# Second layer of the last three token tiles by seven block products in place of eight, with sums of W_out's blocks kept in DRAM

## The chip, the cores and the metric

One core of a Trainium2 chip runs the whole kernel. TensorE (PE in the profile; its weight loads are the row PEld) multiplies, VectorE (DVE), ScalarE (ACT) and GpSimd (POOL) do the rest, and SyncE (SP) and ACT issue the transfers. The metric is the device time of one execution in microseconds, the median of several runs.

## The reference

Block-sparse attention over 4 batches, 8 heads, 768 tokens and 64 features a head, then a feed-forward with two weight matrices on the 3072 x 512 result:

```python
scores = np.where(mask, scale * np.matmul(q, k.transpose(0, 1, 3, 2)), -1e9)   # block mask, 32 x 32 blocks
attn = np.exp(scores - max); attn = attn / (attn.sum(-1, keepdims=True) + 1e-9)
x = np.matmul(attn, v).transpose(0, 2, 1, 3).reshape(3072, 512)
h = x @ w_in                                                     # 512 -> 2048
sp = np.where(h > 20.0, h, np.log1p(np.exp(np.minimum(h, 20.0))))
out = (h * np.tanh(sp)) @ w_out                                  # 2048 -> 512
```

## The kernel before, in words

Attention runs as 52 jobs, 13 a batch: two blocks of 32 queries a job, with a dense job for the first and the last block of a batch. A job's scores (tile s) need its keys gathered by POOL into one of three buffers (kg0 to kg2, L598) and its values gathered by SP from DRAM (vg<-vd); then come maximum, exponential, transposes (t), score-weighted values (obank), a division and a transpose back (tx), and the result is stored in two half-precision parts, xh and xl.

The feed-forward works on 12 tiles of 256 tokens, three a batch, written 0_0 to 3_2. Everything in it is a pair of float16 parts, a high part and a remainder, and a product of two such pairs takes three matmuls (high x high, high x low, low x high). The first layer (`moe_h`, L1049) makes h of a tile in 8 pieces of two steps; a step is 12 matmuls of 256 columns, and its weights change with every matmul. Two pieces make one quarter k of a tile: 512 of the 2048 hidden features, laid out as 4 chunks of 128 on the partitions. The activation (`moe_g`) of a quarter is a chain: two copies of h out of PSUM (hs, ACT L1060), exponential (us, ACT L1078), a minimum and an addition (DVE L1081), a square (POOL L1083 or ACT L1084), a logarithm and an exponential (ACT L1085, L1086), the product with hs (DVE L1087), the cast to float16 (g's high part, DVE L1096 or ACT L1094), and the remainder (POOL L1099).

The second layer (`moe_y`, L1114) takes, for each half m of 128 tokens, the 16 chunks of W_out (`wo`, 512 columns each) times g: 48 matmuls of 512 columns into one PSUM bank, in steps of 6 matmuls; 96 a tile. Then the bank is scaled into ys (DVE or ACT, L1126 and L1128) and sent out (SP, L1132). The second layer of a tile runs between the first-layer steps of the tile that follows; that of the last tile runs alone at the end, first half of the tokens before the second.

The order on every engine is fixed when the program is built, by a planner (`Plan`): each piece of work is added with an engine (or several to choose from), an estimated length, what it reads and writes, and a rank; the planner places them one after the other by these estimates, with rings of buffers as limits (`RINGS`). Semaphores are put in afterwards from the tiles that instructions read and write; in PSUM they keep two engines apart by bank. A step of the feed-forward is ready work for PE whenever an attention step is not; the feed-forward's steps keep their own order. W_out is decoded and split into its two parts before the feed-forward needs it, and stays in SBUF.

Of the kernel before, what the change touches and what calls it, by code (L numbers as in the profile page):

```python
# [21 lines left out]
PSC = 4096.0  # L22
# [186 lines left out]
def attn_mish_kernel(ctx: ExitStack, tc: tile.TileContext, qT, kT, v, sampled, blocks, w_in, w_out, out):  # L209
# [11 lines left out]
    nc = tc.nc  # L221
    P = 128
# [99 lines left out]

    sb = ctx.enter_context(tc.tile_pool(name="attn", bufs=2))
    ps = {n: ctx.enter_context(tc.tile_pool(name=f"ps_{n}", bufs=RINGS[n], space=PSUM)) for n in "sthy"}
# [17 lines left out]
    NKG, NVG = 2, 3  # L342
    kgs = [const.tile([P, 2 * NPR, KT], F16, name=f"kg{n}") for n in range(NKG)]
    vgs = [const.tile([P, 2, H, VW], F16, name=f"vg{n}") for n in range(NVG)]
    RAW = H * VW
    T3 = range(NTT)

    def squares(src, out):

        n = src.free_size()  # L350
        junk = sb.tile([P, 4 * TT], F16, name=nc.get_next_instruction_name(), tag="jk", bufs=1)
        nc.scalar.activation(out=junk[:, 0:n], in_=src, func=AF.Square, scale=float(2.0 ** -SQ), accum_out=out)
# [112 lines left out]
    def parts(b, what, j, cls):  # L465
# [15 lines left out]
        def hi():  # L481
            if first:
                new(sb, "kt", kt, [P, 2 * NPR, S], F16)
            elif what == "q":
                new(sb, "q", key, [P, 2 * NPR, TT], F16)
            raw, h, _ = views()
            nc.scalar.activation(out=h, in_=raw, func=AF.Copy, scale=tl[ks])
# [13 lines left out]
        if (what, b, j) in APART:  # L501
# [7 lines left out]
            def hi_of(eng):  # L509
                if first:  # L510
                    new(sb, "kt", kt, [P, 2 * NPR, S], F16)
                elif what == "q":
                    new(sb, "q", key, [P, 2 * NPR, TT], F16)
# [155 lines left out]
    def attend(job):  # L669
# [52 lines left out]
        def ex_fn(n):  # L722
            if n == 0:
                for k in kps:
                    new(sb, "pt", k, [P, S] if dense else [P, 2, 2, KT])
            pt, nb = tl[kp], tl["nb", i]
# [22 lines left out]
        def ph_fn(j):  # L749
            nc.scalar.activation(out=new(sb, "ph", ("ph", i, j), [P, 2, 2, P], F16), in_=tl["t", i, j], func=AF.Copy,  # L750
                                 scale=PSC)

        def pl_fn(j):
            nc.vector.scalar_tensor_tensor(  # L754
                out=new(sb, "pl", ("pl", i, j), [P, 2, 2, P], F16), in0=tl["t", i, j], scalar=PSC,
                in1=tl["ph", i, j], op0=ALU.mult, op1=ALU.subtract)
# [5 lines left out]
        def plf_fn(j):  # L762
            nc.scalar.activation(out=new(sb, "pl", ("pl", i, j), [P, 2, 2, P], F16), in_=tl["t", i, j], func=AF.Copy,
                                 scale=PSC)
# [40 lines left out]
        def xs_fn():  # L805
# [3 lines left out]
            nc.vector.reciprocal(out=r, in_=r)  # L809
            xs = new(sb, "xs", ("xs", i), [P, nsu, 2, D])  # L810
            nc.vector.tensor_tensor(
# [129 lines left out]
    def add_split(key, kg, a0, hi, lo, r, ring, cls, sc, ks, by_pe):  # L941
# [15 lines left out]
        if not by_pe:  # L957
# [20 lines left out]
            also=[("DVE", 0.68, lambda: cast("DVE", lo), False)])  # L978

    def a0_o(fc):  # L980
        return wo[:, fc].rearrange("p t d -> p (t d)").bitcast(F32)
# [85 lines left out]
    def moe_g(st, k, part):  # L1067

        b, t = st
        kq, ku, kg, kp = ("hs", b, t, k, part), ("us", b, t, k, part), ("g", b, t, k), ("gp", b, t, k, part)  # L1070
        n, c = (TT, 1.0) if part is None else (TT // 2, 0.56)
# [18 lines left out]
        def g_fn(eng):  # L1090
# [8 lines left out]
        add("POOL", 2.3 * c, lambda: nc.gpsimd.tensor_tensor(out=g(1), in0=hs(), in1=g(0), op=ALU.subtract),  # L1099
            r=[kq, ("gh",) + kp], w=[kp], use=[kg])  # L1100

# [35 lines left out]


    DL = 10
    jobs = []  # L1140
# [19 lines left out]
    def open_mlp():  # L1160
        wpool_cm.__exit__(None, None, None)
        pools["cm"] = tc.tile_pool(name="mlp", bufs=2)
        pools["m"] = pools["cm"].__enter__()

    LPE = 4
# [60 lines left out]
    for i, job in enumerate(jobs):  # L1226
# [32 lines left out]
    for st in order + [None]:  # L1259
        ys = [(m, k) for m in range(TT // P) for k in range(NFC // 4)] if prev else []  # L1260
        if st in HALVES:
            for n in range(NFP):
                moe_h(st, n, 0)
        for n in range(NFP):
            if st:
                moe_h(st, n, 1 if st in HALVES else None)
            if ys:
                moe_y(prev, *ys[n], st is None)
        prev = st
# [43 lines left out]
    FILL = 14.0, 200.0  # L1313
    plan.emit(pace, fill)
    pools["cm"].__exit__(None, None, None)

# [41 lines left out]
```

## Time and profile before

| what | value |
|---|---|
| median of 3 runs | 789.04 us (788.4 to 790.24) |
| span of the profiled execution, first to last instruction | 786.6 us |
| the median less that span | 2.4 us |
| instructions | 30628 |
| second-layer matmuls (L1114), 512 columns | 1152 |
| first-layer matmuls (L1049), 256 columns | 2304 |

The page gives the span of the profiled execution and no other time of it; the 2.4 us are what the timed runs hold on top. A busy PE in the profile is not PE at its peak, since matmuls overlap: the mean length of one (380 ns for 512 columns) is longer than the distance from the start of one to the start of the next. Idle time is put down to what ended it.

### The profile page before, as it was taken

What the parts mean: (1) busy time and instruction counts of PE and PEld (TensorE: products, weight loads), DVE (VectorE), ACT (ScalarE), POOL (GpSimd) and SP (SyncE); (2) the same over time, 40 slices, a digit from 0 to 9 for tenths busy, and PEclk for the clock granted to TensorE, in tenths of its full rate; (3) what the DMA queues carried; (4) which work ended last, traced back from release to release, by engine and by line L of the source; (5) the groups of instructions that cost most, each with busy time, mean ns of one, the idle gap of its engine ahead of it and who ended that gap; (6) DMA issues with size and microseconds to landing.
All of it is one profiled execution on the core that took longest, in us unless ns stands there. A gap on an engine that the chain in (4) does not pass through costs nothing.

```text
span 786.6 us, 30628 instructions
## 1 busy us (share of the span) xinstructions
PE 740.5 (94%) x12793; PEld 518.7 (66%) x12793; DVE 493.5 (63%) x900; ACT 542.7 (69%) x880; POOL 307.6 (39%) x393
## 2 busy tenths in 40 slices
PE   6677899888999999999999999999999999999997
PEld 5544578665577767767776676677677667666663
DVE  6868988998767764795866457656665453223220
ACT  3555778768868877777887768786876666455650
POOL 2114244887635542374443422534641331213021
PEclk9989999999999999999999999999999999999999
DMA  9878857104534475244346603523444112000000
GB/s 339 263 236 256 268 176 202 44 2 136 159 117 131 119 198 171 69 162 120 87 139 194 192 15 101 174 77 91 119 115 119 37 39 81 14 15 14 14 14 27
DMA packets 57742, 95.31 MB, mean 121 GB/s; under 512 B 8323, under 2 KB 20612, under 8 KB 57604
## 3 DMA queue, kind: packets, MB, share of 16 engines
q1 hardware_dynamic: 52032, 80.51, 34.9%
q10 hardware_dynamic: 5572, 12.85, 4.8%
q8 instruction: 100, 1.64, 0.9%
q14 instruction: 38, 0.31, 0.1%
HBM read 80.38 MB, written 12.95 MB: 119 GB/s over the span
## 4 chain that ended last, share of the span: by engine, by line
PE 73%; DVE 10%; ACT 6%; DMA 5%; issue 2%; POOL 1%; SPq 1%; POOLq 1%; ACTq 0%; DVEq 0%
PE h_None L1049 27%; PE y L1114 26%; PE obank L789 6%; PE t L667 6%; PE s L661 4%; DMA vg<-vd 3%; PE tx L667 1%; PE wd_i L947 1%; DVE wt_o L965 1%; DMA wr<-in_moe_w_in_dram 1%; DVE hs_None L1087 1%; DVE v L491 1%; DMA raw_k<-in_k_dram 1%; ACT us_None L1078 1%; POOL kt L522 1%
## 5 line engine op out<-in xcount | busy, mean ns | idle before, releaser
L1049 PE MATMUL h_None<-xh,wi 128*128 128x256 f16 x1536 | 282.8, 273 | 0.0
L1114 PE MATMUL y<-wo,g 128*128 128x512 f16 x1152 | 278.0, 380 | 4.0 <-POOL wo L970 2.6
L1049 PEld LDWEIGHTS <-wi 128*128 128x128 f16 x2304 | 223.5, 98 | 47.3 <-issue 2.1
L1049 PE MATMUL h_None<-xl,wi 128*128 128x256 f16 x768 | 209.8, 273 | 0.0
L1114 PEld LDWEIGHTS <-g 128*128 128x128 f16 x1152 | 111.1, 98 | 106.7 <-issue 7.3
L1099 POOL TENSOR_TENSOR g<-hs_None,g 128x1024 f16<-128x1024 f32 x48 | 107.6, 2241 | 188.4 <-DVE g L1096 144.8
L598 POOL COPY kg<-kt 128x256 f16 x258 | 107.2, 451 | 123.3 <-PE s L661 109.7
L1060 ACT ACTIVATE hs_None<-h_None,gsc 128x512 f32<-128x512 f32 x96 | 65.5, 684 | 80.2 <-PE h_None L1049 79.4
L727 ACT ACTIVATE pt<-s,nb,ns 128x256 f32<-128x256 f32 (+1 forms) x208 | 106.3, 582 | 5.7 <-PE t L667 5.0
L750 ACT ACTIVATE ph<-t 128x512 f16<-128x512 f32 x112 | 66.5, 596 | 45.1 <-PE t L667 45.0
L754 DVE SCALAR_TENSOR_TENSOR pl<-t,ph 128x512 f16<-128x512 f32 x105 | 71.9, 686 | 35.8 <-ACT ph L750 35.5
L1087 DVE SCALAR_TENSOR_TENSOR hs_None<-us_None,hs_None 128x1024 f32<-128x1024 f32 x48 | 65.0, 1355 | 40.1 <-ACT us_None L1086 40.1
L667 PE MATMUL t<-ident,pt 128*128 128x128 f32 x448 | 70.4, 280 | 6.8 <-DVE pl L754 3.6
L708 DVE TENSOR_REDUCE mx<-s 128x4 f32<-128x1024 f32 x44 | 53.7, 1222 | 31.9 <-PE s L661 31.3
L1083 POOL TENSOR_TENSOR us_None<-us_None 128x1024 f32<-128x1024 f32 x22 | 44.2, 2007 | 71.8 <-DVE us_None L1081 68.7
L667 PEld LDWEIGHTS t<-ident,pt 128*128 128x128 f32 x448 | 51.6, 142 | 21.4 <-DVE pl L754 4.5
L789 PEld LDWEIGHTS <-ph 128*32 128x32 f16 x3584 | 47.9, 94 | 20.9 <-issue 13.1
L1078 ACT ACTIVATE us_None<-hs_None,hsc 128x1024 f32<-128x1024 f32 x48 | 55.2, 1150 | 0.9
L789 PE MATMUL obank<-vg,ph 128*32 128x65 f16 (+1 forms) x3200 | 50.6, 196 | 4.0 <-DMA vg<-vd 2.2
L1081 DVE TENSOR_SCALAR us_None<-us_None 128x1024 f32<-128x1024 f32 x48 | 37.4, 778 | 25.4 <-ACT us_None L1078 25.2
L1085 ACT ACTIVATE us_None<-us_None 128x1024 f32<-128x1024 f32 x48 | 50.7, 1056 | 1.6 <-POOL us_None L1083 0.8
L1086 ACT ACTIVATE us_None<-us_None 128x1024 f32<-128x1024 f32 x48 | 50.7, 1056 | 0.8
(199 smaller groups left out, 893.6 us busy)
## 6 DMA issues: line engine op xcount, KB each, us to landing
vg<-vd SPq DMA_DIRECT2D x320, 65.0 KB, 2.6
vg<-vd SPq DMA_DIRECT2D x80, 195.0 KB, 3.2
wr<-in_moe_w_in_dram ACTq DMA_DIRECT2D x8, 1024.0 KB, 7.4
vd<-v SPq DMA_DIRECT2D x12, 520.0 KB, 3.8
vg<-vd SPq DMA_DIRECT2D x12, 520.0 KB, 5.1
raw_k<-in_k_dram SPq DMA_DIRECT2D x12, 512.0 KB, 5.4
raw_q<-in_q_dram SPq DMA_DIRECT2D x12, 512.0 KB, 4.3
raw_v<-in_v_dram SPq DMA_DIRECT2D x12, 512.0 KB, 5.0
```

The lines of the kernel that those rows point to most:

```text
L598: nc.gpsimd.tensor_copy(out=dst, in_=tl["kt", b][:, :, ds(j, BS)])
L667: nc.tensor.matmul(out, src, ident, start=start, stop=stop, is_transpose=True)
L727: ex = lambda o, x, g, w: nc.scalar.activation(out=o, in_=x, func=AF.Exp, bias=nb[:, g, w:w + 1], scale=tl["ns", b, sus[w]["qb"] // TB][:, ...
L750: nc.scalar.activation(out=new(sb, "ph", ("ph", i, j), [P, 2, 2, P], F16), in_=tl["t", i, j], func=AF.Copy, scale=PSC)
L754: nc.vector.scalar_tensor_tensor(out=new(sb, "pl", ("pl", i, j), [P, 2, 2, P], F16), in0=tl["t", i, j], scalar=PSC, in1=tl["ph", i, j], op ...
L789: nc.tensor.matmul(o[cs, w, g, 0:v1 - v0], p[:, k, g, cs], vt[:, k, 2 * c + g, v0:v1], start=j == 0 and g == 0 and k == 0 and n == 0, stop ...
L1049: nc.tensor.matmul(h[:, f2, 0:n].rearrange("p (s q) -> p s q", q=BS), wi[:, fp, cc // 2, w, cc % 2, fs], x[:, s0:s0 + sn, cc], start=f2 == ...
L1060: nc.scalar.activation(out=tl[kq][:, 2 * (fp % 2):2 * (fp % 2) + 2, 0:n], in_=tl[kh][:, :, 0:n], func=AF.Copy, scale=gsc[:, fp:fp + 1])
L1078: nc.scalar.activation(out=us(), in_=hs(), func=AF.Exp, scale=hsc[:, b:b + 1])
L1087: add("DVE", 1.32 * c, lambda: nc.vector.scalar_tensor_tensor(out=hs(), in0=us(), scalar=-0.5, in1=hs(), op0=ALU.add, op1=ALU.mult), r=[ku ...
L1099: add("POOL", 2.3 * c, lambda: nc.gpsimd.tensor_tensor(out=g(1), in0=hs(), in1=g(0), op=ALU.subtract), r=[kq, ("gh",) + kp], w=[kp], use=[kg])
L1114: nc.tensor.matmul(tl[ky], tl["g", b, t, k][:, g, f, q], wo[:, fc, w], start=fc == 0 and n == 0, stop=fc == NFC - 1 and n == 2)
```

## The change

For the last three tiles, 3_0, 3_1 and 3_2, the second layer is done by a scheme with seven products of blocks for eight. Of each quarter k, g is a 2 x 2 arrangement of blocks (two halves of 128 tokens by two halves of 256 features), and so is W_out (two halves of 256 features by two halves of 256 columns). Seven products of one block each, some of them of sums of blocks, give the four output blocks after additions. A product is 6 matmuls of 256 columns (two chunks, three pairs of parts), 42 a quarter and 168 a tile. Each of the seven gathers over all four quarters in its own half of a PSUM bank; the banks are those of y, s and obank for tiles 3_0 and 3_1, and those of h and t for tile 3_2. Two products share a bank in three of four cases.

The sums of W_out's blocks are made once, while jobs 27 to 41 of attention run: for each of 8 pairs of chunks two additions on DVE, four on POOL (or DVE), a cast to the high part and a subtraction for the low part, and a store of 512 KB to DRAM by SP. When attention is over, its buffers are given up and a pool in their place (`late`) takes the sums back with 8 transfers (`to`). The sums of g's blocks (`sg`) are made for each quarter behind the activation chain: four additions into the tile us, a cast, a subtraction. For these three tiles the remainder of g and both steps of sg may go to DVE as well as to POOL or ACT. When the last quarter is through, the seven products are scaled and added into yz by two copies on ACT and seven instructions on DVE or POOL, in place of two scalings, and each half of the tokens is sent out as before. The steps of second and first layer are mixed in proportion to their estimated lengths. The key and value buffers of attention, and other tiles of it, move to a pool on the other side of SBUF; nothing else about them is changed. First layers are as they were.

```diff
+        if not fold:
+            return
+        ksg = ("sg", b, t, k)
+        def fold_g(eng):
+            x = lambda f, m: tl[kq][:, 2 * f:2 * f + 2, m * P:(m + 1) * P]
+            y = [tl[ku][:, n].rearrange("p (j q) -> p j q", j=2) for n in range(4)]
+            for o, a_, b_, op in ((S1, x(0, 1), x(1, 1), ALU.add), (S3, x(0, 0), x(0, 1), ALU.subtract),
+                                  (S2, y[S1], x(0, 0), ALU.subtract), (S4, x(1, 0), y[S2], ALU.subtract)):
+                eng.tensor_tensor(out=y[o], in0=a_, in1=b_, op=op)
+        add("DVE", 1.4, lambda: fold_g(nc.vector), r=[kq], w=[ku], port=True,
+            also=[("POOL", 2.5, lambda: fold_g(nc.gpsimd), True)])
...
+    NLATE, WHEN = 3, [27, 28, 29, 30, 31, 32, 40, 41]
+    PRODS = ((B11, None, B11, None), (B12, None, B21, None), (None, S1, None, F1), (None, S2, None, F2),
+             (None, S4, B22, None), (None, S3, None, F3), (B22, None, None, F4))
+    HL = ((0, 0), (1, 0), (0, 1))
+    def folded(rk, r, four, two, parts, keys, home, after, use=(), ring="ft", rush=0.0, free=()):
+        def sums():
+            for o, a, b in four:
+                nc.vector.tensor_tensor(out=o(), in0=a(), in1=b(), op=ALU.add)
+        def fold(eng):
+            x = [r()[:, n] for n in range(4)]
+            for o, a, b, op in two:
+                eng.tensor_tensor(out=x[o], in0=x[a], in1=x[b], op=op)
...
+        add("SP", 0.5, lambda: nc.sync.dma_start(out=folds[key], in_=flat(kt).bitcast(F16)),
+            r=[("fh",) + key, ("fl",) + key], w=[("fd",) + key], use=[kt], lat=2.5, kind=dma(2.0), key=8.0)
...
+    def back_wo(k, j):
+        kt = ("to", k, j)
+        add("SP", 0.5, lambda: nc.sync.dma_start(
+            out=new(pools["l"], "to", kt, [P, 2, 4, TT], F16).rearrange("p w t f -> p (w t f)"), in_=folds["o", k, j]),
+            r=[("fd", "o", k, j), "late"], w=[("toh", k, j)], new=[("to", kt)], lat=2.5, kind=dma(2.0), key=-2 + k)
+
+    def pair_y(st, final):
+        sets = [("h", 0), ("h", 1), ("t", 0), ("t", 1)] if final else [("y", 0), ("s", 0), ("s", 1), ("o", 0)]
...
+        where = {0: (0, 0), 1: (0, 1), 2: (1, 0), 3: (1, 1), 5: (2, 0), 4: (2, 1), 6: (3, 0)}
+        R = lambda i: bank(where[i][0])[:, where[i][1] * TT:(where[i][1] + 1) * TT]
+        seq_ = (0, 3, 1, 2, 5, 4, 6)
+        def product(k, i, head):
+            a, s_, bb, t_ = PRODS[i]
+            for j in range(2):
+                for n, (x, w) in enumerate(HL):
+                    if a is not None:
+                        lhs = tl["g", b, t, k][:, x, 2 * (a % 2) + j, (a // 2) * P:(a // 2 + 1) * P]
+                    else:
+                        lhs = tl["sg", b, t, k][:, x, s_, j * P:(j + 1) * P]
+                    rhs = wo_at(4 * k + j + 2 * (bb // 2))[:, w, (bb % 2) * TT:(bb % 2 + 1) * TT] if bb is not None else \
+                        tl["to", k, j][:, w, t_]
+                    nc.tensor.matmul(R(i), lhs, rhs, start=head and j == n == 0,
+                                     stop=k == NFC // 4 - 1 and j == 1 and n == 2, skip_group_check=True)
+        for k in range(NFC // 4):
+            for i in seq_ if k < NFC // 4 - 1 else (0, 3, 2, 5, 4, 6, 1):
...
+        def end():
+            copy(0, 0, 0)
+            acc(3, 0, 1, 0, 0)
+            copy(2, 1, 1)
+            acc(5, 1, 0, 0, 1)
+            both(0, 1, 1, 1)
+            both(1, 1, 1, 0)
+            acc(4, 0, 1, 0, 1)
+            acc(6, 1, 0, 1, 0)
+            out_(1)
+            acc(1, 0, 0, 0, 0)
+            out_(0)
...
+    late_ = order[len(order) - NLATE:]
+    plain = order[:len(order) - NLATE + 1]
+    add("SP", 0.0, open_late, r=[("xw", i) for i in range(nj)], w=["late"], key=-9)
...
+    for st in order[len(plain):] + [None]:
+        steps, end = pair_y(prev, st is None)
+        ys = [(0.66, x) for x in steps[:-1]] + [(0.66, lambda s_=steps[-1], e=end: (s_(), e()))]
+        mixed([(2.62, lambda n=n, st=st: moe_h(st, n, None)) for n in range(NFP)] if st else [], ys)
```

More of the change, by code (lines that the diff above doesn't have):

```diff
@@ L749, in ph_fn @@
         def ph_fn(j):
-            nc.scalar.activation(out=new(sb, "ph", ("ph", i, j), [P, 2, 2, P], F16), in_=tl["t", i, j], func=AF.Copy,
+            nc.scalar.activation(out=new(at_, "ph", ("ph", i, j), [P, 2, 2, P], F16), in_=tl["t", i, j], func=AF.Copy,
                                  scale=PSC)
@@ L1135, in moe_y @@
             add("SP", 0.4, out_fn, r=[kys], lat=2.0, kind=("dma", 1.1))
+    dma = lambda d, n=1: ("dma", d)
+    NLATE, WHEN = 3, [27, 28, 29, 30, 31, 32, 40, 41]
+    B11, B12, B21, B22 = range(4)
+    F1, F3, F4, F2 = range(4)
+    S2, S4, S3, S1 = range(4)
+    PRODS = ((B11, None, B11, None), (B12, None, B21, None), (None, S1, None, F1), (None, S2, None, F2),
[9 more added lines that the diff above has]
+                eng.tensor_tensor(out=x[o], in0=x[a], in1=x[b], op=op)
+        out = lambda n: parts()[n]
+        add("DVE", 1.3, sums, r=after, w=[rk], new=[(ring, rk)], use=use, key=rush)
+        add("DVE", 1.35, lambda: fold(nc.vector), w=[rk], use=[rk], key=rush, port=True,
+            also=[("POOL", 2.4, lambda: fold(nc.gpsimd), True)])
+        add("ACT", 1.07, lambda: nc.scalar.activation(out=out(0), in_=r(), func=AF.Copy), r=[rk, *free],
+            w=[keys[0]], new=home, use=[rk, *keys[2:]], key=rush, also=[("DVE", 0.75, lambda: nc.vector.tensor_copy(out=out(0), in_=r()), True)])
+        add("DVE", 1.2, lambda: nc.vector.tensor_tensor(out=out(1), in0=r(), in1=out(0), op=ALU.subtract), port=True,
+            r=[rk, keys[0]], w=[keys[1]], use=[rk, *keys[2:]], key=rush,
+            also=[("POOL", 2.25, lambda: nc.gpsimd.tensor_tensor(out=out(1), in0=r(), in1=out(0), op=ALU.subtract), True)])
@@ new lines, in attn_mish_kernel, with fold_w, flat @@
+    FOLD_W = ((F1, B12, B11, ALU.subtract), (F3, B22, B12, ALU.subtract), (F2, B22, F1, ALU.subtract),
+              (F4, B21, F2, ALU.subtract))
+    folds = {}
+    def fold_w(key, four, when):
+        kr, kt = ("fr",) + key, ("ff",) + key
+        folds[key] = dram.tile([P, 8 * TT], F16, name="_".join(str(x) for x in ("folds",) + key))
+        def flat(k):
+            return tl[k] if k in tl else new(sb, "raw", k, [P, RAW], cols=4 * TT)
+        r = lambda: flat(kr).rearrange("p (n f) -> p n f", n=4)
+        parts = lambda: [flat(kt).bitcast(F16).rearrange("p (w n f) -> p w n f", w=2, n=4)[:, n] for n in range(2)]
+        folded(kr, r, [(lambda o=o: o(r()), a, c) for o, a, c in four], FOLD_W, parts, [("fh",) + key, ("fl",) + key, kt],
+               [("raw", kt)], [(w, key[0], *at) for w in ("wh", "wl") for at in (
+                   [(key[1], n) for n in range(2)] if key[0] == "i" else [(4 * key[1] + key[2] + 2 * h,) for h in range(2)])] +
+               [("begun", when)], (), "raw", 8.0)
+        add("SP", 0.5, lambda: nc.sync.dma_start(out=folds[key], in_=flat(kt).bitcast(F16)),
+            r=[("fh",) + key, ("fl",) + key], w=[("fd",) + key], use=[kt], lat=2.5, kind=dma(2.0), key=8.0)
@@ L1163, in open_mlp, with open_late @@
         pools["m"] = pools["cm"].__enter__()
+    def open_late():
+        at_cm.__exit__(None, None, None)
+        pools["lcm"] = tc.tile_pool(name="late", bufs=2, side="right", reuse_waits="tile")
+        pools["l"] = pools["lcm"].__enter__()
     LPE = 4
```

137 lines of the change are left out of this document (116 added, 21 removed).

## The prediction

> **What bounds the kernel now.** I read the page first (busy shares and the slices), then a table by stage, the timeline of the last 27 us, and the waits of TensorE. The page:
>
> ```profile
> PE 740.5 (94%) x12793; PEld 518.7 (66%) x12793; DVE 493.5 (63%) x900; ACT 542.7 (69%) x880; POOL 307.6 (39%) x393
> ```
>
> A table by stage says more than the 94%. Columns: stretch, its length, busy time with instruction count of PE, PEld, DVE, ACT and POOL, granted clock, DMA share, GB/s.
>
> ```profile
> 380.00:600.00 220.00, 217.12 (x4237) 155.21 (x4226) 141.00 (x268) 168.27 (x286) 91.88 (x139) 1.00 0.42 119
> 600.00:666.00 66.00, 65.52 (x982) 45.47 (x981) 29.59 (x50) 41.41 (x62) 14.87 (x12) 1.00 0.25 69
> 666.00:759.60 93.60, 93.60 (x649) 63.30 (x647) 25.55 (x30) 50.80 (x55) 21.93 (x10) 1.00 0.04 12
> 759.60:786.60 27.00, 22.19 (x103) 9.72 (x100) 3.27 (x4) 6.38 (x7) 2.12 (x1) 0.96 0.08 29
> ```
>
> From 666 us, when attention is over, to 759.6 PE has not one idle moment, at full clock, while DVE is at 27%, ACT at 54% and POOL at 23%. From 380 to 600 PE idles 2.9 of 220 us. So from there to the end the time is PE's instruction stream, and whatever shortens it, with its operands on time, shortens the run one for one. The end itself (start, length, engine, line, operation; in brackets the idle time before and who ended it):
>
> ```profile
> 759.33 0.27 PE L1049 MATMUL h_None<-xh,wi 128*128 128x256 f16 x1
> 759.44 9.66 PE L1114 MATMUL y<-wo,g 128*128 128x512 f16 x44
> 759.64 0.69 ACT L1060 ACTIVATE hs_None<-h_None,gsc 128x512 f32<-128x512 f32 x1 [3.98 <-PE h_None L1049]
> 760.36 1.15 ACT L1078 ACTIVATE us_None<-hs_None,hsc 128x1024 f32<-128x1024 f32 x1
> 761.61 0.68 DVE L1081 TENSOR_SCALAR us_None<-us_None 128x1024 f32<-128x1024 f32 x1
> 762.32 1.06 ACT L1084 ACTIVATE us_None<-us_None 128x1024 f32<-128x1024 f32 x1 [0.81 <-DVE us_None L1081]
> 765.66 1.23 DVE L1087 SCALAR_TENSOR_TENSOR hs_None<-us_None,hs_None 128x1024 f32<-128x1024 f32 x1 [3.37 <-ACT us_None L1086]
> 767.78 2.12 POOL L1099 TENSOR_TENSOR g<-hs_None,g 128x1024 f16<-128x1024 f32 x1 [8.28 <-DVE g L1096]
> 769.96 12.69 PE L1114 MATMUL y<-wo,g 128*128 128x512 f16 x58 [0.86 <-POOL g L1099]
> 782.74 0.69 ACT L1126 ACTIVATE ys<-y,osc 128x512 f32<-128x512 f32 x1 [9.72 <-PE y L1114]
> 783.45 0.33 SPq L1132 DMA_DIRECT2D out_dram<-ys  x1
> ```
>
> The last first-layer matmul ends at 759.60; the activation chain of the last quarter of g takes until 769.90, and PE, which reaches that quarter of the first token half at 769.10, waits 0.86 us for it. Then PE runs to 782.65, one eviction ends at 783.43, and the last transfer fills the time to 786.6.
>
> **The change, part by part.** (1) Second-layer matmuls. Removed: 3 tiles x 96 = 288 of 512 columns. Added: 3 x 4 quarters x 7 products x 6 = 504 of 256 columns. The price of the first: 58 in a row take 12.69 us, the last of them 0.38 by its group's mean; (12.69 - 0.38) / 57 = 0.216 us from start to start. The price of the second is that of the first layer, the same shape with new weights for every matmul:
>
> ```profile
> 128.01 2.62 PE h_None L1049 x24
> 667.12 1.31 PE h_None L1049 x12
> 727.03 1.31 PE h_None L1049 x12
> L1114 PE MATMUL y<-wo,g 128*128 128x512 f16 x1152 | 278.0, 380 | 4.0 <-POOL wo L970 2.6 <-POOL g L1099 0.9 <-ACT wo L968 0.5
> ```
>
> 24 in 2.62 us on the chain is 0.109 each. The pair of 12 first-layer and 6 second-layer matmuls repeats 23 times between 667.12 and 727.03, 2.605 us each; less 6 x 0.216 leaves 1.309, again 0.109. So 288 x 0.216 = 62.2 us become 504 x 0.109 = 55.0: **-7.2 us**, all on the path.
>
> (2) The wait of 0.86 us. In the change the last tile's products go quarter by quarter, so PE comes to the last quarter later, but the chain gets longer: four additions of 128x256 on hs, a cast and a subtraction for the sums of g (the tile sg). DVE's queue at the end, before, and in the change (us, hs, g: the activation's tiles of tile 3_2 by quarter; yr: the product banks; yz: the output tile):
>
> ```order
> L1128 TENSOR_SCALAR ys_3_1_1_19143<-y_3_1_1_18972,osc_82 128x512
> L1081 TENSOR_SCALAR us_3_2_3_None_19134<-us_3_2_3_None_19134 128x1024
> L1087 SCALAR_TENSOR_TENSOR hs_3_2_3_None_19090<-us_3_2_3_None_19134,hs_3_2_3_None_19090 128x1024
> L1096 CAST g_3_2_3_19175<-hs_3_2_3_None_19090 128x1024
> L1354 UNCONDITIONAL_BRANCH
> ```
>
> ```order
> L1118 TENSOR_TENSOR us_3_2_3_None_19481<-hs_3_2_3_None_19416,us_3_2_3_None_19481 128x256
> L1107 TENSOR_TENSOR g_3_2_3_19582<-hs_3_2_3_None_19416,g_3_2_3_19582 128x1024
> L1131 TENSOR_TENSOR sg_3_2_3_19597<-us_3_2_3_None_19481,sg_3_2_3_19597 128x1024
> L1303 SCALAR_TENSOR_TENSOR yz_3_2_19648<-yr_3_2_1_19492,osc_82,yz_3_2_19648 128x256
> L1303 SCALAR_TENSOR_TENSOR yz_3_2_19648<-yr_3_2_2_19516,osc_82,yz_3_2_19648 128x256
> L1308 TENSOR_TENSOR yz_3_2_19648<-yz_3_2_19648 128x256 x2
> L1303 SCALAR_TENSOR_TENSOR yz_3_2_19648<-yr_3_2_2_19516,osc_82,yz_3_2_19648 128x256
> L1303 SCALAR_TENSOR_TENSOR yz_3_2_19648<-yr_3_2_3_19524,osc_82,yz_3_2_19648 128x256
> L1303 SCALAR_TENSOR_TENSOR yz_3_2_19648<-yr_3_2_0_19483,osc_82,yz_3_2_19648 128x256
> ```
>
> The subtraction of g moved from POOL to DVE, that of sg follows it, and after them stand seven small instructions that assemble the output. Prices of the unseen forms come from these groups (operation, tiles, shape, count, busy us, mean ns):
>
> ```profile
> L811 DVE TENSOR_TENSOR xs<-obank,r 128x256 f32<-128x256 f32 x44 | 18.7, 424 | 1.5
> L876 DVE SCALAR_TENSOR_TENSOR wo<-wor,wo 128x512 int32<-128x512 int32 x16 | 11.4, 722 | 0.0
> L873 DVE TENSOR_SCALAR wo<-wor 128x512 int32<-128x512 int32 x16 | 6.8, 444 | 0.0
> L598 POOL COPY kg<-kt 128x256 f16 x258 | 107.2, 451 | 123.3 <-PE s L661 109.7 <-POOL kg L598 9.1 <-issue 2.1
> L970 POOL TENSOR_TENSOR wo<-wt_o,wo 128x512 f16<-128x512 f32 x16 | 22.6, 1421 | 7.7 <-DVE wo L969 6.4 <-DVE tp_k L394 1.0 <-ACT wo L968 0.3
> ```
>
> A 128x256 on DVE: 0.42 us; a two-input 128x1024 on DVE: 1.23, the L1087 row. Counted from the end T of the first layer: hs stands at T+7.3 (765.66 + 1.23 less 759.60), +0.3 because ACT puts the 1.06 us cast of the third quarter before its square; four additions to T+9.3; g's subtraction to T+10.5; sg's to T+11.8. After T PE still has two products of the tile before and 21 of three quarters, 23 x 6 x 0.109 = 15.0 us. The last quarter is ready 3 us early: **-0.86 us**.
>
> (3) The end. The last product ends at E; DVE's third-last group starts when the last product but two is done (E-1.3), and six instructions of 0.42 us end at E+1.25, where the one eviction ended at E+0.78: **+0.5**. The last two transfers, 256 KB each, now go out within half a microsecond; nothing to 0.8 us (256 KB at the page's best slice):
>
> ```profile
> GB/s 339 263 236 256 268 176 202 44 2 136 159 117 131 119 198 171 69 162 120 87 139 194 192 15 101 174 77 91 119 115 119 37 39 81 14 15 14 14 14 27
> out_dram<-ys SPq DMA_DIRECT2D x24, 256.0 KB, 2.2
> raw_k<-in_k_dram SPq DMA_DIRECT2D x12, 512.0 KB, 5.4
> ```
>
> I take the middle, **+0.4**.
>
> (4) Blocks that share a bank. At the end of tiles 3_0 and 3_1 two products write two halves of one bank, and the first half is read before the second product starts. DVE's queue there, with what each waits for:
>
> ```order
> L1131 TENSOR_TENSOR sg_3_1_1_18887<-us_3_1_1_None_18788,sg_3_1_1_18887 128x1024 [waits Activation_49]
> L1087 TENSOR_SCALAR us_3_1_2_None_18909<-us_3_1_2_None_18909 128x1024 [waits Activation_49]
> L1303 SCALAR_TENSOR_TENSOR yz_3_0_18924<-yr_3_0_1_18574,osc_82,yz_3_0_18924 128x256 [waits PE_49,Activation_49]
> L1303 SCALAR_TENSOR_TENSOR yz_3_0_18924<-yr_3_0_1_18574,osc_82,yz_3_0_18924 128x256 [waits Activation_49]
> L1308 TENSOR_TENSOR yz_3_0_18924<-yz_3_0_18924 128x256 [waits Pool_49]
> ```
>
> The first yz instruction releases PE's next product; ahead of it, the next tile's us waits for ACT. PE has one first-layer step of 1.31 us in between as cover. By the rows it is hs 0.69, exponential 1.15, us 0.68 and the 0.42 itself, 2.9 us from the first-layer step that feeds them, and up to two subtractions of 1.23 stand in front; PE has four products and two steps, 5.2 us, till it wants the bank. That is about even. Lowest price 0; highest, DVE late by the worst delay its group shows, twice:
>
> ```profile
> L1087 DVE SCALAR_TENSOR_TENSOR hs_None<-us_None,hs_None x48: 1207/1225/3144, 127.0 to 765.7; 128x1024 f32<-128x1024 f32 x48
> ```
>
> 3.14 - 1.23 = 1.9, so 3.8 in all. The median is near the minimum, so I take **+0.4**. The Trainium skill, page "PSUM — Partial Sum Buffer", section "PSUM bank collisions raise a hardware error", says that a read by another engine and a write by TensorE must be kept apart by bank even at different columns. By that rule this wait is there for good; without it the term would be 0. No row of the trace before shows two such blocks.
>
> (5) Making the sums of W_out, between 380 and 600 us: 16 additions of 128x512 on DVE (0.44 to 0.72 each), 32 of 128x256 and 8 of 128x1024 on POOL (0.45 to 0.71, half a row of L970, and 2.1), 8 casts on ACT (1.1), 8 stores of 512 KB. That is about 1.2 + 2.3 + 2.1 + 1.1 = 6.7 us per pair of chunks, 54 in all, in engines that are busy 401 us in that stretch. None is on PE; PE's own work covers it. POOL's queue at the first, before and now (kg0, kg1: gathered key blocks that the scores wait for; fr, ff: sums and their two parts):
>
> ```order
> L598 COPY kg1_111<-kt_2_9545 128x8x32
> L1099 TENSOR_TENSOR g_1_1_0_10400<-hs_1_1_0_None_9719,g_1_1_0_10400 128x1024
> L1099 TENSOR_TENSOR g_1_1_1_10466<-hs_1_1_1_None_10089,g_1_1_1_10466 128x1024
> L598 ISA
> L598 COPY kg0_110<-kt_2_9545 128x8x32
> ```
>
> ```order
> L600 COPY kg1_114<-kt_2_9556 128x8x32
> L1105 TENSOR_TENSOR g_1_1_0_10412<-hs_1_1_0_None_9730,g_1_1_0_10412 128x1024
> L1189 TENSOR_TENSOR fr_o_0_0_10377<-fr_o_0_0_10377 128x256 x4
> L1198 TENSOR_TENSOR ff_o_0_0_10629<-fr_o_0_0_10377,ff_o_0_0_10629 128x1024
> L600 ISA
> L600 COPY kg0_113<-kt_2_9556 128x8x32
> ```
>
> The gather now waits behind 4.4 us of sums, which wait for DVE and ACT. The scores stand correspondingly later in PE's list: job 30's come after seven more first- and second-layer steps of 1.3 us than before, so PE has something else meanwhile. 401 us beside 2.9 us of PE idle makes 54 us worth **+0.4**; the ends are -2.9 (all that idle gone, since the list is new) and 36 (8 x 4.5 us, all exposed).
>
> (6) Reading the sums back: 8 transfers of 512 KB on SP once attention is over. PE then still has 8 first-layer and 7 second-layer steps, 20 us, before the first product that needs one, and about 10 per quarter after; at 5.4 us one by one each pair is early. 0.
>
> Sum: -7.2 - 0.86 + 0.5 + 0.4 + 0.4 + 0.4 = **-6.4 us**. The span of 786.6 becomes 780.2; the median lies 2.4 above the span, so **782.7 us**.
>
> **The rivals.** *Late evictions* (4): DVE runs behind in tiles 3_0 and 3_1, and PE waits at the shared banks. For: DVE gains 44 additions and 18 assembling instructions of 0.42 us and 19 subtractions of 1.23 and gives 14 casts of 0.7 to ACT, about 40 us; against: from 29 it comes to 69 of 118 us. At 3.8 us the time is 786.1. *Sums ahead of gathers* (5), which ends slower: POOL and DVE hold each other up, gathers come late, and PE stands at scores. For: DVE's 3144 beside a median of 1225, and the queue above. Against: among PE's waits from 200 us on, none at the scores is ended by POOL:
>
> ```profile
> PE obank L789 <- DMA vg<-vd: 2.2, 2, 1.2
> PE s L661 <- issue: 1.2, 2, 0.9
> PE y L1114 <- POOL g L1099: 0.9, 1, 0.9
> ```
>
> It takes 6.8 / 8 = 0.85 us of PE wait per pair of chunks to undo the gain; at one POOL subtraction each (2.1) it is 789.0 - 6.8 + 17 = 799, at 1.2 about 792. The Trainium skill, page "SBUF — State Buffer", section "Who interferes with whom", calls the port that VectorE and GpSimd share an exclusive lock. The 3144 agrees: the median plus nearly one POOL instruction. *More idle gone*: the new list also loses the 2.9 us of 380 to 600: 779.4. *No fewer PE cycles*: the small products cost more than the first layer's matmuls; at 0.123 us each (62.2 / 504) (1) is nothing, and 789.9 is left.
>
> **How the numbers follow.** Forecast 0.64; late evictions 0.14; sums ahead of gathers 0.08; more idle gone 0.08; no fewer cycles 0.06. The likeliest case alone spans 780.5 to 785. The range, 779.2 to 787.4, takes in late evictions and most of the better case, and leaves out the slower ones. A change below 0.2%, 1.6 us, can't be told from none: faster 0.84 (forecast, more idle gone, nearly all late evictions), same 0.09, slower 0.07.
>
> **What would show it.** Right: 504 matmuls of 256 columns at 0.109 us from start to start; PE busy throughout after attention; no wait before the last quarter; about 1.3 us from PE's last matmul to the last DVE instruction. Wrong: PE idle before products and ended by DVE (4), before scores and ended by POOL, or before the score-weighted values and ended by a gather that queued behind a store on SP (5), or ended by a transfer of sums (6).

## The result, and the profile after

The changed kernel takes 784.0 us (median of 16 runs; 788.5 for the kernel before beside it): a ratio of 0.994, 95% interval 0.9925 to 0.9959, or 3.2 to 5.9 us less. A repeat gave 0.996 (0.9937 to 0.9987). Forecast were 782.7 us, 6.3 below the first median: faster was right, and the gain was put somewhat too high, since 6.3 lies just outside the interval. The ratios leave out three executions far above the others of their kernel (797.3 and 945.6 us of the kernel before, 1222.0 us of the last kernel in the table below). The profiled execution took 782.35 us with a span of 780.3; that of the kernel before had a span of 786.6, so the profiles differ by 6.3 us where the medians differ by 4.5.

The page of the changed kernel, busy time and instructions of each engine:

```profile
PE 734.3 (94%) x13009; PEld 540.2 (69%) x13009; DVE 558.9 (72%) x984; ACT 574.0 (74%) x916; POOL 345.0 (44%) x430
```

The table by stage (columns as in the prediction):

```profile
380.00:600.00 220.00, 216.42 (x4206) 154.26 (x4212) 157.00 (x273) 178.91 (x294) 127.25 (x166) 1.00 0.44 133
600.00:666.00 66.00, 64.41 (x1111) 45.60 (x1097) 35.06 (x64) 42.03 (x67) 18.69 (x21) 1.00 0.39 118
666.00:753.00 87.00, 86.92 (x768) 74.89 (x766) 53.59 (x77) 63.80 (x72) 11.48 (x6) 1.00 0.08 32
```

After attention PE works almost without a break, as forecast (86.92 of 87). Between 380 and 666 us, where the sums of W_out are made, it now idles 3.58 + 1.59 = 5.2 us; before, 2.88 + 0.48 = 3.4. The end (start, length, engine, line, operation, idle time before):

```profile
774.09 0.48 DVE L1303 SCALAR_TENSOR_TENSOR yz<-yr,osc,yz 128x256 f32<-128x256 f32 x1 [0.77 <-PE yr L1266]
774.55 0.82 PE L1266 MATMUL yr<-wo,g 128*128 128x256 f16 x6
774.68 0.89 DVE L1308 TENSOR_TENSOR yz<-yz 128x256 f32<-128x256 f32 x2
775.49 1.26 DVE L1303 SCALAR_TENSOR_TENSOR yz<-yr,osc,yz 128x256 f32<-128x256 f32 x3
776.38 0.81 SPq L1315 DMA_DIRECT2D out_dram<-yz  x2
```

PE ends at 775.37, DVE 1.4 us later (an eviction 0.78 later before), the span 4.9 after PE (3.9 before).

The start of a run varies by a microsecond or two, so from here on profiles are also compared over the stretch from PE's 6,501st instruction (196.5 us in the kernel before; small matmuls that an experiment adds ahead of it are not counted, so the same point of the work begins it everywhere) to the end. That row for the kernel before, and for the changed one:

```profile
196.48:786.70 590.22, 578.74 (x9557) 401.33 (x9555) 329.54 (x590) 409.66 (x647) 218.67 (x280) 1.00 0.34 98
```

```profile
197.37:780.40 583.03, 570.96 (x9773) 422.18 (x9771) 394.93 (x674) 441.15 (x683) 256.30 (x317) 1.00 0.37 113
```

216 matmuls more (504 - 288), and 7.8 us less work on PE, at full clock in both. The matmuls' gain is all there; what is missing from the total has to be idle time, or lie ahead of this stretch.

### The profile page after: what moved, and what is told of

Read it like the earlier page. It is cut to its first block, busy times and chain, and to the rows that moved or that the text cites. A ratio compares the mean times of both kernels' runs of the same rounds, so it can differ in the third digit from the quotient of the medians.

```text
span 780.3 us, 31241 instructions
## 1 busy us (share of the span) xinstructions
PE 734.3 (94%) x13009; PEld 540.2 (69%) x13009; DVE 558.9 (72%) x984; ACT 574.0 (74%) x916; POOL 345.0 (44%) x430
## 3 DMA queue, kind: packets, MB, share of 16 engines
q8 instruction: 102, 1.67, 0.9%
## 4 chain that ended last, share of the span: by engine, by line
PE 70%; DVE 11%; DMA 6%; issue 5%; ACT 4%; SPq 3%; POOL 0%; ACTq 0%; DVEq 0%; POOLq 0%
PE h_None L1054 25%; PE y L1145 21%; PE t L669 6%; PE obank L791 6%; PE yr L1266 5%; PE s L663 5%; DMA vg<-vd 2%; DMA vd<-v 1%; PE tx L669 1%; DVE wt_o L967 1%; SPq L624 1%; DVE v L493 1%; PE wd_i L949 1%; DVE hs_None L1093 1%; DMA raw_q<-in_q_dram 1%
## 5 line engine op out<-in xcount | busy, mean ns | idle before, releaser
L1145 PE MATMUL y<-wo,g 128*128 128x512 f16 x864 | 211.1, 381 | 3.1 <-POOL wo L972 2.6
L600 POOL COPY kg<-kt 128x256 f16 x258 | 112.3, 469 | 115.5 <-PE s L663 101.8
L1145 PEld LDWEIGHTS <-g 128*128 128x128 f16 x864 | 82.9, 99 | 78.6 <-issue 7.2
L1105 POOL TENSOR_TENSOR g<-hs_None,g 128x1024 f16<-128x1024 f32 x38 | 86.6, 2281 | 59.4 <-DVE g L1102 28.5
L1089 POOL TENSOR_TENSOR us_None<-us_None 128x1024 f32<-128x1024 f32 x19 | 39.4, 2076 | 71.7 <-DVE us_None L1087 71.7
L1087 DVE TENSOR_SCALAR us_None<-us_None 128x1024 f32<-128x1024 f32 x48 | 40.8, 850 | 13.8 <-ACT us_None L1084 13.7
```

What stands on the lines that cost most here:

```text
L600: nc.gpsimd.tensor_copy(out=dst, in_=tl["kt", b][:, :, ds(j, BS)])
L1145: nc.tensor.matmul(tl[ky], tl["g", b, t, k][:, g, f, q], wo[:, fc, w], start=fc == 0 and n == 0, stop=fc == NFC - 1 and n == 2)
```

## The experiments

All runs in one table. "Change" is the ratio of times times 788.5 us, less 788.5, with its 95% interval; PE's work and idle time are those of the stretch just shown, in one profile each (the idle time includes the 4 to 5 us after PE's last matmul, and up to 0.2 us of rounding at the end of the stretch). Two profiles of the same changed kernel differ by 1.7 us of idle time, 12.1 and 13.8; a smaller difference between two rows is not shown by one profile each.

| kernel | change, us | PE work | PE idle |
|---|---|---|---|
| before | 0 | 578.7 | 11.5 |
| changed | -4.5 (-5.9 to -3.2) | 571.0 | 12.1 |
| changed, again | -3.0 (-5.0 to -1.0) | 571.8 | 13.8 |
| sums made, not used | +3.3 (+1.5 to +5.2) | 578.5 | 13.7 |
| changed, no sums | -5.3 (-7.2 to -3.4) | 571.1 | 13.9 |
| seven products in the last tile only | -0.2 (-1.9 to +1.5) | 576.1 | 12.2 |
| before, 68 small matmuls | +10.2 (+6.5 to +13.9) | 578.7 | 15.0 |
| changed, 56 small matmuls | -3.6 (-5.7 to -1.6) | 571.2 | 11.6 |
| changed, seven banks | -4.8 (-7.0 to -2.6) | 571.2 | 13.3 |
| before, last tile by quarters | -0.1 (-2.0 to +1.8) | 578.1 | 10.1 |
| changed, 56 in the gap | -6.1 (-8.0 to -4.3) | 570.4 | 11.2 |
| sums not used, 56 in the gap | +1.4 (-0.7 to +3.6) | 578.6 | 13.9 |
| changed, seven tiles | -5.8 (-8.8 to -2.9) | 571.4 | 10.6 |
| changed, both | -6.9 (-9.4 to -4.5) | 571.2 | 10.0 |

**First: what the sums cost, and what a tile is worth.** Four kernels: the change again; sums without use; use without the sums' arithmetic; one tile instead of three.

> The changed kernel once more, as the mark for the other runs of this chip. Both theories: 4.5 us below the kernel before (3.2 to 5.9), as first timed; in the profile no idle moment of PE from 666 to 753 us, products 0.109 us from start to start, and about 5 us of idle PE from 200 to 666 us (5.2 in the first profile, 5.6 - 0.9 at other places in the kernel before). If the few pauses of 1 to 1.6 us in mid run (541, 546 and 638 us) belong to the change, they stand at the same places again; if they are chance, they stand elsewhere.

> Computes the whole result with the eight products of the kernel before for every tile, but makes the sums of W_out at the same jobs and stores them; nobody reads them. So it shows term 5 (making the sums) alone. Theory A (the sums lie beside PE's work, and the 7.2 us of matmuls came nearly whole): 0 to +2 us against the kernel before. Theory B (the matmuls and the end gave more than 8 us together and the sums took 3 us or more of it back): +3 us or more, with idle PE at scores or in the score-weighted values between 380 and 640 us.

```diff
-    late_ = order[len(order) - NLATE:]
-    plain = order[:len(order) - NLATE + 1]
+    late_ = []
+    plain = order + [None]
...
-            back_wo(k, j)
```

> The changed kernel, but in place of the sums two parts of W_out as they stand are stored and read back: the additions, casts and subtractions of W_out's sums on DVE, POOL and ACT are left out, the transfers and all products stay. Its output is therefore not the reference's. Theory A: 0 to 2 us below the changed kernel, that is 4.5 to 6.5 below the kernel before. Theory B: 3 us or more below the changed kernel, 7.5 or more below the kernel before. If the stores rather than the arithmetic disturb PE, this run is like the changed kernel and the run with the sums alone is slower than before.

```diff
...
+        add("SP", 0.5, lambda: nc.sync.dma_start(
+            out=folds[key].rearrange("p (h w d) -> p h w d", h=2, w=2), in_=wo[:, fc:fc + 3:2]),
...
-        fold_w(("o", k, j), [(o(h), lambda h=h: wo_at(fc(h))[:, 0], lambda h=h: wo_at(fc(h))[:, 1]) for h in range(2)], when)
```

> The seven products for the last tile alone; the two tiles before it with eight, as in the kernel before; all sums made as in the change. Theory A (2.4 us for each tile by PE's matmuls, from 62.2 - 55.0 us over three tiles): 4.8 us slower than the changed kernel, so about the time of the kernel before (-1 to +1.5), its profile with 192 products of 512 columns more. Theory C (the gain is made at the end of the program, where the wait for the last quarter of g went, and the small products are hardly cheaper): at most 2 us slower than the changed kernel, 2.5 or more below the kernel before.

```diff
-    NLATE, WHEN = 3, [27, 28, 29, 30, 31, 32, 40, 41]
+    NLATE, WHEN = 1, [27, 28, 29, 30, 31, 32, 40, 41]
```

The seven products are worth what PE's matmuls say: PE's work falls from 578.7 by 2.6 us with one tile and by 7.0 to 7.8 with three. By the times, one tile instead of three is 4.3 us slower beside the changed kernel as first timed and 2.8 beside the repeat on the same chip (theory A: 4.8; C: at most 2); the intervals are too wide to rule C out, PE's work does. Making the sums, alone, costs 3.3 us (1.5 to 5.2), near the border that theory B had set; the interval takes in A's 2. Yet leaving their arithmetic out gains only 0.8 to 2.3 us: theory B's 3 is not there either. Neither theory had the cause. PE's waits from 380 to 666 us (engine, tile and line that waited, releaser: total us, times, longest), in the kernel before and with the sums alone:

```profile
PE s L661 <- issue: 1.2, 2, 0.9
PE obank L789 <- issue: 1.0, 2, 0.6
PE obank L789 <- DMA vg<-vd: 1.0, 1, 1.0
```

```profile
PE s L663 <- issue: 3.0, 3, 1.6
PE obank L791 <- issue: 2.5, 3, 1.3
PE tp_q L389 <- DVE pl L756: 1.0, 1, 1.0
PE obank L791 <- DVE pl L756: 0.3, 1, 0.3
```

No POOL, no gather: 5.5 us of the 6.8 shown end with "issue", time in which PE waits for nothing that the profile shows. The rows themselves, in the changed kernel and in its repeat:

```profile
541.26 0.19 PE L791 MATMUL obank<-v,ph 128*32 128x64 f16 x1 [1.60 <-issue]
637.83 0.27 PE L663 MATMUL s<-kg,q 64*32 64x256 f16 x1 [1.59 <-issue]
```

```profile
543.36 0.19 PE L791 MATMUL obank<-v,ph 128*32 128x64 f16 x1 [1.56 <-issue]
640.17 0.27 PE L663 MATMUL s<-kg,q 64*32 64x256 f16 x1 [1.58 <-issue]
```

The same two instructions, the same length: not chance. Where are they in PE's list? The table by stretch, cut at the pause, counts PE's matmuls and weight loads up to it, here for the changed kernel and its repeat:

```profile
0.00:541.20 541.20, 503.04 (x9634) 358.43 (x9635) 413.35 (x737) 412.09 (x686) 276.48 (x354) 0.98 0.51 157
0.00:637.80 637.80, 596.89 (x11663) 425.58 (x11664) 475.61 (x860) 484.11 (x811) 321.05 (x416) 0.99 0.49 150
```

```profile
0.00:543.30 543.30, 503.88 (x9634) 359.61 (x9635) 413.22 (x737) 412.18 (x686) 276.41 (x354) 0.98 0.52 156
```

With the queue's own instructions, which these counts leave out, the first pause is ahead of instruction 19,393 = 75 x 256 + 193 and the second ahead of 23,489 = 91 x 256 + 193. In the kernel before, the pause at 643.7 us stands at 23,489 too, that at 477.1 at 17,601 = 68 x 256 + 193. Over all fourteen profiles there are 56 pauses of more than 0.3 us after 200 us that end with "issue", and every one stands at 193 or 194 (a weight load or its matmul). The page of the changed kernel names what comes in such blocks; its columns are queue, packets, MB, share:

```profile
q8 instruction: 102, 1.67, 0.9%
```

1.67 MB in 102 packets is 16 KB each, and PE's list of 26,191 instructions over 102 is 257: a packet is a block of 256 instructions of 64 bytes. The one of the pause at 541.26 starts between 538.6 and 538.7 us (that window holds just this row), 0.4 us after PE began the block before, takes 1.2, and PE goes on 1.4 us after it has landed:

```profile
q8 instruction: 1, 0.02, 75.9%
```

Most blocks last longer than these 3 us. One that holds little but the attention's small matmuls can be over sooner, and PE stands till the next is there: ahead of 39 of the 56 pauses PE had run a block in 1.3 to 3.4 us. A short block alone is not enough, though. Of the 145 blocks that were run in 3.4 us or less after 200 us in the fourteen profiles, only these 39 were followed by such a pause; the packet of the next block had then begun 0.9 us after the short block did (median), and 1.0 us ahead of it at the 106 others. What decides when a packet begins is not shown. The Trainium skill, page "Runtime: NRT & Kernel Launch", section "Instruction fetch mechanics", has the blocks (16 KiB, 256 instructions) as the trace shows them, and calls their cost mostly hidden; here, in the changed kernel, four pauses between 515 and 638 us make 4.5 us.

**Second: move the blocks, not the work.** Theory D is that the pauses belong to where the blocks fall. A few small matmuls without use, 68 in the kernel before and 56 in the changed one, shift every block behind them:

```diff
+        if a > 175.0 and not at["open"] and "shift" not in at:
+            at["shift"] = 1
+            for k in range(68):
+                nc.tensor.matmul(obank[0:32, NO:NO + 16], neg[:, 0, 0:32], neg.rearrange("p n q -> p (n q)")[:, 0:16],
+                                 start=True, stop=True)
```

> The kernel before, with 68 small matmuls of 16 columns (136 instructions of PE with their weight loads, results unused) put where PE waits 3.6 us for DVE at 176 us; everything else in the same order. In the six profiles so far each longer pause of PE that ends with 'issue' stands at a matmul or weight load whose number in PE's list leaves 193 when divided by 256, about 1.3 us after a 16 KB packet of the DMA queue 'q8 instruction' has landed. Theory D: PE's list arrives in blocks of 256 instructions; a block that holds little but the attention's small matmuls is run in 2 to 3 us, less than the 3.65 us from the request of the next to its use, and PE pauses for the rest; which jobs are hit depends on the number of instructions ahead. A replay of the recorded starts with blocks 136 instructions later gives 7.3 us of pauses after 205 us (at about 223, 321, 368, 524, 540 and 638 us of the old time) for 1.9 as it stands: +3 to +6 us. Theory B (the pauses come with the work on the sums or their transfers): 0, since the small matmuls lie in idle time.

> The changed kernel with 56 such small matmuls at the same place, so that its blocks begin 112 instructions later in the work. Theory D: the pauses at 515, 541, 546 and 638 us (4 us in all) go, new ones of 0.3, 0.8, 0.3 and 1.2 us come at about 225, 321, 368 and 484 us: 0.5 to 2 us below the changed kernel, with 1.2 us or less of such pauses after 380 us. Theory B: the same pauses at the same jobs, and the same time.

The kernel before gets 10 us slower, where 3 to 6 were expected. Its pauses after 205 us now stand at the six block edges that the replay had named, and one more at 219 us. (The instructions at these edges begin at 227, 325, 373, 531, 547 and 646 us in the kernel before, 4 to 8 us later than the replay had them; the pause at the second, 331 us here, is under 0.3 us.)

```profile
231.97 0.28 PE L661 MATMUL s<-kg,q 64*32 64x256 f16 x1 [1.58 <-issue]
380.27 0.83 PE L661 MATMUL s<-kg,q 64*32 64x256 f16 x43 [1.35 <-issue]
537.12 0.28 PE L661 MATMUL s<-kg,q 64*32 64x256 f16 x1 [1.59 <-issue]
553.80 0.28 PE L661 MATMUL s<-kg,q 64*32 64x256 f16 x2 [0.38 <-issue]
652.36 0.28 PE L1049 MATMUL h_None<-xh,wi 128*128 128x256 f16 x1 [0.72 <-issue]
```

The count of PE's instructions up to the third of them, again from the table by stretch:

```profile
0.00:537.10 537.10, 496.02 (x9634) 354.63 (x9634) 389.91 (x727) 392.68 (x664) 235.44 (x318) 0.98 0.51 152
```

The pause at 537.12 stands at a score matmul, another job in another kernel than the 541.26 above, but at the same block edge of the list (75 x 256 + 193). The one at 477 is gone. From the 6,501st instruction of the work on, this profile is 3.5 us longer, all of it idle; rows that end with "issue" make 6.6 us, for 2.2 in the kernel before. Theory B's 0 is out. The small matmuls cost another 1.9 us, because I had put them at the wrong place: they ran when PE was busy.

```profile
L1314 PE MATMUL obank<-neg x68: 168/169/183, 189.8 to 191.5; 128*32 128x16 f16 x68
```

That makes 5.4 of the 10; the profiled execution was the fastest of the six timed, and what the others spent more is not shown. In the changed kernel the pauses moved as well (228, 325, 445, 491 and 568 us, none left at 515 to 546 or 638), and the time stayed: -3.6 for -4.5 and -3.0, with 1.6 us paid for the small matmuls. That is no clear gain where 0.5 to 2 us were expected, and after 380 us the pauses make 2.8 us, not 1.2 or less. Of the four places named, the one at 368 us had no pause; those at 445 and 568 us were not forecast. The packet for the pause at 445 us started 4.3 us after the block before began, in a stretch where data filled the transfer engines (window 440 to 444 us of that profile: their busy tenths in 40 slices, and the queues):

```profile
DMA  9999798897999989898989798879936689966875
q1 hardware_dynamic: 550, 1.16, 93.9%
q8 instruction: 1, 0.02, 1.6%
```

The other profiles have the same. Of the 1,064 packets after 200 us, 86 started more than 2.5 us after the block before began, and in each case data took at least 44% of the transfer engines between the two starts; 11 of the 56 pauses follow such a packet, behind blocks that had lasted 4.9 to 6.1 us. So a block can be late because the one before it is short, or because its packet comes late beside data. No run here moves the data away, so the second is seen and not tested. Six pauses, the one at 546.26 us of the changed kernel among them, are neither: a block of 4.0 us, its successor's packet 2.3 us late, and no data beside it. Why that packet is late is not shown.

**The end of the program.** Two kernels in the same comparison:

> The changed kernel with a bank for each of the last tile's seven products (of the seven, three pairs shared a bank before). The order of the work is the same. If the end is set by DVE's last six small instructions, which begin when the third-last product is read (1.4 us from PE's last matmul to DVE's end), they can start one product earlier: 0.6 to 0.8 us less from PE's last matmul to the end of the span, and as much in the time. If the two last transfers set the end (256 KB each, 0.5 us apart), the first of them leaves earlier and the second as before: 0 to 0.3 us.

```diff
-        sets = [("h", 0), ("h", 1), ("t", 0), ("t", 1)] if final else ...
+        sets = [("h", 0), ("h", 0), ("t", 0), ("t", 0), ("s", 0), ("s", 1), ("y", 0)] if final else ...
```

> The kernel before with the last tile's second layer taken quarter by quarter, both token halves in turn, with its eight products: term 2 alone. The wait of 0.86 us for the last quarter of g goes; both evictions now come at the end, 0.69 us each on one engine, and both transfers: -0.9 to 0 us, no other difference. If the 0.86 us was hidden anyway, or the end costs as much, 0.

```diff
+        if st is None:
+            ys = [(m, k) for k in range(NFC // 4) for m in range(TT // P)]
```

Seven banks changed nothing at the end: 24.9 us from the start of the last first-layer matmul to the end of the span, as in the changed kernel. By quarters, PE has no wait left after 666 us, and that stretch is 26.5 us (785.4 - 758.9) where it was 27.3 (786.6 - 759.3):

```profile
L1049 PE MATMUL h_None<-xh,wi x1536: 269/273/417, 103.1 to 758.9; 128*128 128x256 f16 x192
```

0.8 us in the profile, as term 2 said. The comparison of times (-2.0 to +1.8) can't tell it from nothing. Its order of work up to 666 us is that of the kernel before, yet rows that end with "issue" make 0.8 us here and 2.2 there: the pauses of one list vary by more than a microsecond from one execution to the next.

**Third: small matmuls in the real gap, and seven tiles.**

> The changed kernel with the 56 small matmuls of the run before put one place earlier, where PE really waits 3.6 us for DVE (in that run they stood ten us later and cost 1.6 us of busy PE). Theory D: from the place of the small matmuls to attention's end 2.8 us less than the changed kernel, as in the last run's profile, and the matmuls themselves free: about 2.8 us below the changed kernel, 7 to 8 below the kernel before. Rival (where the blocks fall was only this one profile's chance): no more than 1 us below the changed kernel, and pauses at other places than in the last run (228, 325, 444, 491 and 567 us).

> Eight products for every tile as in the kernel before, the sums of W_out made and stored for nobody, and 56 small matmuls in PE's idle gap. With the blocks where they fell, this cost 2.6 to 3.4 us against the kernel before. Theory D: most of that goes: 0 to +1.2 us against the kernel before. Theory B (the work of the sums or their stores holds PE up): +2.5 us or more, as without the small matmuls.

```diff
-        if a > 175.0 and not at["open"] and "shift" not in at:
+        if a > 167.5 and not at["open"] and "shift" not in at:
```

> The changed kernel with the last tile's seven products in seven tiles of one bank each. In the run with seven banks, two products still lay in one tile of two banks, and DVE's read of the first waited for the end of the second (776.58 where the first ended about 775.9), so that nothing was gained at the end. Here that read waits for its own product alone. If that is what holds the end: PE's last matmul to DVE's end 0.5 us for 1.4, and the last tile 0.6 to 0.9 us shorter from the last first-layer matmul to the end of the span (24.9 before). If the two transfers, 0.5 us apart, hold it: 0.3 us or less.

```diff
+        sets = [("h", 0), ("h", 0), ("t", 0), ("t", 0), ("s", 0), ("o", 0), ("y", 0)] if final else ...
+        kb = [("yr", b, t, n) for n in range(len(sets))]
```

> Both together: seven tiles at the end and 56 small matmuls in the idle gap. If theory D and the first reading of the end hold: 3.5 us below the changed kernel, about 8 below the kernel before. If neither: as the changed kernel.

In the gap the small matmuls are free. Waits of PE from 380 to 666 us in the changed kernel with 56 of them there:

```profile
PE s L663 <- issue: 1.2, 1, 1.2
PE y L1145 <- issue: 0.4, 1, 0.4
```

1.6 us where the changed kernel has 4.7 in rows that end with "issue"; two more pauses, at 228 and 325 us, take 1.8 back. The kernel is 1.6 us faster than the changed one by the ratios (3.1 than the repeat), where 2.8 were expected; the intervals of the two overlap (-8.0 to -4.3 and -5.9 to -3.2), so the gain in time is likely, not shown. The places were right but for 568 us, where no pause came.

With the sums alone theory D did not hold: the pauses moved (235, 332, 452, 498 and 575 us), but PE's idle time stayed, 13.9 for 13.7 us. +1.4 (-0.7 to +3.6) lies just above D's 0 to 1.2, below B's 2.5, and not apart from the +3.3. The trace has both halves: from the 6,501st instruction on, rows that end with "issue" fall from 5.5 to 3.8 us, as D said, and waits for other engines and for transfers rise from 3.8 to 5.7. Two profiles of the changed kernel differ by 1.2 us in such waits (2.0 and 3.3), so part of the rise can be chance; one profile each can't tell how much.

Seven tiles did at the end what seven banks had not:

```profile
773.73 0.48 DVE L1304 SCALAR_TENSOR_TENSOR yz<-yr,osc,yz 128x256 f32<-128x256 f32 x1 [0.77 <-PE yr L1267]
774.32 0.89 DVE L1309 TENSOR_TENSOR yz<-yz 128x256 f32<-128x256 f32 x2
774.84 0.82 PE L1267 MATMUL yr<-wo,g 128*128 128x256 f16 x6
775.12 0.48 DVE L1304 SCALAR_TENSOR_TENSOR yz<-obank,osc,yz 128x256 f32<-128x256 f32 x1
775.52 0.86 DVE L1304 SCALAR_TENSOR_TENSOR yz<-yr,osc,yz 128x256 f32<-128x256 f32 x2
```

The read that led DVE's last group comes 1.1 us before PE's last product starts (0.5 before), DVE ends 0.7 us after PE instead of 1.4, and the last tile takes 24.2 us instead of 24.9. Both edits together have the lowest ratio to the kernel before, 0.9912 (0.9881 to 0.9943), 6.9 us less where about 8 were expected. Its interval still overlaps that of the changed kernel; what speaks for it are the two mechanisms, each seen in its rows.

## Why the prediction was right, term by term

The forecast of 782.7 was 1.3 us from the median; faster was right, and the mechanism, less work on PE at its price, was the one seen. That the forecast span of 780.2 met the profile's 780.3 is luck in part: PE's work fell by 0.6 us more than forecast, the stretch behind the 6,501st instruction began 0.9 us later, terms 4 and 5 missed in opposite directions, and the span of the repeat's profile was 782.7. By its terms:

(1) **Matmuls, -7.2**: right. PE's work in the stretch is 7.0 to 7.8 us less in three profiles of the changed order, and one tile alone 2.6. Six small matmuls start every 0.655 us, 0.109 each. "No fewer PE cycles" is out.

(2) **Last quarter of g, -0.86**: right. The wait is gone, and taken alone it is worth 0.8 us of a profile. The margin was smaller than worked out: the last sums of g are done at 769.08 us, 1.5 us before PE comes to that quarter at 770.62, and not 3.

(3) **The end, +0.9**: right, +1.0 (4.93 after PE's last matmul for 3.94): DVE 0.6 us later than the one eviction was, the transfers 0.4 longer. The reason given for DVE was only half right: it waited for the second product of a tile as well.

(4) **Shared banks, +0.4 (0 to 3.8)**: 0 in the changed kernel, so the 0.4 was too much. The wait exists, though: without the sums, with another order around it, PE stood 1.67 us at one such bank, about the 1.9 that had been the bound for one.

```profile
720.84 0.81 PE L1270 MATMUL yr<-wo,g 128*128 128x256 f16 x6 [1.67 <-DVE yz L1307]
```

(5) **Making the sums, +0.4**: this is the term that was mis-sized. Alone it costs 3.3 us (1.4 with its blocks elsewhere, not told apart). In the changed kernel PE idles 0.6 to 2.3 us more than before although the 0.86 of term 2 went and only 1.0 came at the end, so 0.5 to 2.2 are left for this term, by two profiles and one of the kernel before. I had asked who would hold PE up, and weighed POOL, DVE and gathers. The sums took 64.9 us of those engines instead of 54, and even that stayed hidden (groups of the changed kernel: count, busy us, mean ns):

```profile
L1189 POOL TENSOR_TENSOR fr_o<-fr_o 128x256 f32<-128x256 f32 x32 | 26.3, 823 | 2.6 <-DVE fr_o L1184 0.8
L1198 POOL TENSOR_TENSOR ff_o<-fr_o,ff_o 128x1024 f16<-128x1024 f32 x8 | 17.5, 2192 | 2.9 <-ACT ff_o L1194 2.9
L1184 DVE TENSOR_TENSOR fr_o<-wo 128x512 f32<-128x512 f16 x16 | 12.7, 835 | 0.0
L1194 ACT ACTIVATE ff_o<-fr_o 128x1024 f16<-128x1024 f32 x8 | 8.4, 1050 | 1.0 <-POOL fr_o L1189 1.0
```

What came instead is that a new order of work puts other jobs at the edges of PE's 256-instruction blocks: from the 6,501st instruction on, rows that end with "issue" make 4.7 and 5.0 us in the two profiles of the changed kernel, 5.5 with the sums alone, 2.2 before and 2.5 without the sums' arithmetic. Waits for other engines and for transfers went the other way, from 4.0 (without the 0.86 of term 2) to 2.0 and 3.3. A row of this kind was in the profile of before ("PE s L661 <- issue: 1.2, 2, 0.9" was quoted, among the waits), and no term was made of it. That kernel was well placed: shifted by 136 instructions, its list has 6.6 us of such rows.

(6) **Reading back, 0**: right; the loads were issued from 657.4 us on, and no product waited for one.

Of the rivals, *sums ahead of gathers* was wrong in its place: no wait at scores ends with POOL, in any profile of this order. But the stretch that it named, 380 to 640 us, is where time was lost: PE idles 2.3 to 2.7 us more there than before. *More idle gone* was wrong in sign. *Late evictions* did not come here; one such wait, 1.67 us, came in the order without the sums' arithmetic.

## What to carry to other kernels

When PE's work is right and the time is not, count the idle rows that end with "issue" and number their instructions: if they all have one remainder by 256, the list's blocks are the cause, and some sixty small matmuls in an idle gap show it; here they moved every pause, but that they made a kernel faster is only likely. A reordered kernel moves these edges even where the work is the same, so a change of 2 to 5 us is only known after the pauses of both lists have been compared. And give each product that is read on its own a tile of its own, not only a bank.

## What the hardware showed that I had not expected

PE's list arrives in 16 KB packets of 256 instructions, each begun about when the block before begins (median 0.9 us after, 3.1 before to 4.5 after); from the packet's start to use it took 2.2 to 2.9 us at the pauses. A block of small matmuls and weight loads that is run in 1.3 to 3.4 us can outrun it, by up to 1.8 us a time. The 86 packets that began more than 2.5 us late all did so beside data that took 44% of the transfer engines or more.

The time of one kernel goes with the granted clock of its run: over 224 executions of all these kernels, each kernel taken by itself, the span falls by 0.52 us (0.43 to 0.62) for each 0.001 of mean clock, which ranged from 0.98 to 0.995. In the profiles shown the clock was 1.00 in every stage from 200 us to 753, so the difference probably lies at the start and the end of the program. It is part of why comparisons of two to five microseconds stayed as wide as they are here.
